# Attention output computed transposed, reciprocals by ln and exp, a modulation spread by matmuls, and a new order: a one-core adaLN block with sliding attention and an MLP

## The chip, the cores and the metric

The kernel runs on one core of a Trainium2 chip. The metric is the device time in microseconds (us) of one execution. TensorE is called PE, VectorE DVE, ScalarE ACT, GpSimd POOL and SyncE SP. SP mostly issues DMAs; ACT issues a few at the start.

## The reference

```python
mod = (_silu(c) @ w_mod).reshape(c.shape[0], 6, 1, -1)
sa, ca, ga, sb, cb, gb = ...
h = _layernorm(x) * (1 + ca) + sa
x = x + ga * _A_ref(h, A_wqkv, A_wo)
h = _layernorm(x) * (1 + cb) + sb
x = x + gb * _B_ref(h, B_w1, B_b1, B_w2, B_b2)

# _A_ref: H = 16 heads of 28; token s looks at the 8 keys s, s-2, ..., s-14
logits = jnp.einsum('bhsd,bhswd->bhsw', q, kg) * scale
attn = _softmax(jnp.where(mask, logits, -1000000000.0))
o = jnp.einsum('bhsw,bhswd->bhsd', attn, vg)        # then o @ wo
# _B_ref: layernorm, gelu(y @ w1 + b1) @ w2 + b2
```

x is 2048 tokens by 448, in bf16; the MLP is 1792 wide. `c` is one row of 448, so the six modulation vectors sa to gb are one row of 448 each.

## The kernel before

**Layout.** Tokens are split by parity, which turns the dilation of 2 into a plain window of 8 within each half of 1024 tokens. They lie in 16 blocks of 128. `hT` (`T.h`) holds the normalized input transposed, with 448 features in four overlapping slices of 128 rows, so that a product over 448 is three full matmuls and one over 64 rows; `pair_mm` (L592 full, L598 half) does two outputs at a time. `qT` and `kT` hold Q and K transposed, each head on a strip of 32 partitions (28 used), four heads m to a slice.

**First norm.** For each pair of blocks: statistics on DVE (L513 to L516), the power -1/2 on POOL (L520), normalization on DVE into `z` (L531). Blocks 0 to 3 are transposed on PE (L547), blocks 4 to 15 by DMA transposes on SP's queue (L539). `modulate` (L564 on ACT, L567 on DVE) then applies 1 + ca and sa.

**Attention.** Q and K come by chunks of 256 or 512 tokens (L592, L598) and are copied out of PSUM by ACT or DVE (L277, L279). Queries go in 36 groups of 57 tokens, four to one of nine rounds called duos. For each duo: 64 logit matmuls (`lt`, L663), four exponentials on ACT (`ex`, L673), two mask multiplies on DVE (`mk`, L680), V for its keys (`v`, L705 and L714) copied on ACT (`ve`, L277), then 64 value matmuls (`pv`, L739) of 29 columns, of which the 29th, a column of ones beside V, gives the sum of the weights. Queries stand on the partitions of that result. DVE takes reciprocals of the sums (`on`, L750) and multiplies (L752); eight transposes on PE (`pt`, L763) and a copy (`ote`, L277 or L279) bring the result back to features by tokens, into `qT`, whose queries are no longer needed. `wo_pair` multiplies two blocks by `wo`, which was scaled by `ga` (L953), and DVE adds x (L796).

**Second half.** Per pair of blocks: statistics and norm, modulation (`g2`, `sb`), statistics and norm again, all on DVE (L814 to L845) with powers on POOL (L822), then a DMA transpose into `hT` (L853). The MLP goes by quarters of 512 tokens: `w1_pairs` (L592, L598 with `w`), gelu on ACT (L880), and `w2_block` (L893, L899). `w2` was scaled by `gb` (L957), and `xp` on POOL (L808) prepares the sum with x. The output is written by DMA (L920).

**The later modulation.** ga, sb, 1 + cb and gb are rows of one PSUM result (`m2`, L932), each repeated on 32 partitions; DVE copies it to `mrow` (L939), and 16 DMAs on SP's queue (L945) spread each row over 128 partitions.

**What sets the order.** Every step is an `Item` with a cost, the engines it may run on, and the buffers it takes from pools (eight PSUM banks `ps`, three exponential buffers `et` and so on). `Plan.schedule` places the items one after another by priorities: a bias and a slope per kind of step, and a table `delta` of single corrections. Each engine then runs its list strictly in that order; waits are by semaphores. Fillers (`fill`, L456) are matmuls on zeros that keep PE busy. A weight load with `lag=3` waits for the load that stands three places ahead of it. Phases are laid out as attention rounds 0 to 6, MLP quarters 0 and 1, rounds 7 and 8, quarters 2 and 3, with ACT's exponentials and gelus kept apart by phase, since they use different tables.

## Time and profile before

| what | value |
|---|---|
| median of 3 runs | 188.39 us (187.07 to 190.14) |
| the profiled execution | 189.24 us, its span 187.5 us |
| mean granted PE clock in it | 0.951 |
| PE busy | 174.8 us, 93% of the span |
| DVE, ACT, POOL busy | 124.2, 92.7, 38.9 us |
| DMA | 16.17 MB moved, 26630 packets |

The profile's busy share of PE counts matmuls at whatever clock was granted, so a slice at half clock looks as full as one at full clock; the row PEclk tells them apart. A mean over the span mixes three stages: the front (to about 18 us), attention (to 87 us, where the first MLP matmul starts) and the rest, in which MLP quarters and the last two attention rounds are woven. The chain of waits names, step by step, what the last instruction waited for; "issue" in it is time that no wait explains, and SPq is SP's sequencer issuing a DMA.

### The profile page before, as it was taken

The numbers are of one execution on the slowest core, as the hardware profiler recorded it, in microseconds if no ns is written. First come the engines' busy times: TensorE is split into PE (matmuls) and PEld (weight loads), VectorE is DVE, ScalarE is ACT, GpSimd is POOL, SyncE is SP. The second block draws the span as 40 slices with busy tenths as digits, with TensorE's granted clock in tenths as the row PEclk, the third lists the DMA queues.
The fourth block names the chain that finished last, engine by engine and source line by source line (L and its number), as shares of the span: only waits on it lengthen the run. The fifth ranks groups of instructions, "written<-read, shape, count | busy, mean of one in ns | idle before, by whom it ended". The sixth has DMA issues, their size and how long they took to land.

```text
span 187.5 us, 5167 instructions
## 1 busy us (share of the span) xinstructions
PE 174.8 (93%) x2151; PEld 85.3 (46%) x2151; DVE 124.2 (66%) x347; ACT 92.7 (49%) x171; POOL 38.9 (21%) x66
## 2 busy tenths in 40 slices
PE   7699998967799999998999999999999999999992
PEld 2445553432224455563344554355554455434562
DVE  4386997676599699999998986006769985200121
ACT  3055927645278876666570405678541720066400
POOL 7211310300061006411311146002203235000000
PEclk9979999995559999999999999999999999999998
DMA  5999999764820200013022120600000042120011
GB/s 176 349 337 329 224 243 164 242 200 100 141 56 3 56 9 0 3 31 31 2 56 56 23 36 7 150 3 0 3 5 0 0 115 77 22 98 0 0 52 49
DMA packets 26630, 16.17 MB, mean 86 GB/s; under 512 B 16045, under 2 KB 26606, under 8 KB 26606
## 3 DMA queue, kind: packets, MB, share of 16 engines
q1 hardware_dynamic: 25918, 14.92, 33.2%
q10 hardware_dynamic: 688, 0.92, 1.5%
q8 instruction: 17, 0.28, 0.6%
q14 instruction: 7, 0.06, 0.1%
HBM read 9.87 MB, written 1.84 MB: 62 GB/s over the span
## 4 chain that ended last, share of the span: by engine, by line
PE 72%; DMA 11%; DVE 6%; SPq 5%; issue 3%; ACT 1%; DVEq 0%
PE ps L592 31%; PE ps L893 21%; PE ps L598 6%; DMA w<-in_B_w_dram 4%; PE ps L705 3%; DMA hm<-in_w_mod_dram 3%; SPq L945 3%; DMA hT<-z 2%; DMA hT<-y 2%; PE ps L739 2%; PE ps L456 2%; DVE st L513 2%; PE ps L663 2%; PE ps L763 2%; PE ps L899 1%
## 5 line engine op out<-in xcount | busy, mean ns | idle before, releaser
L880 ACT ACTIVATE hm<-ps,b1c 128x512 bf16<-128x512 f32 x56 | 34.1, 689 | 45.5 <-PE ps L598 40.6
L893 PE MATMUL ps<-w,hm 128*128 128x448 bf16 x210 | 41.2, 353 | 0.0
L592 PE MATMUL ps<-hT,w 128*128 128x512 bf16 x168 | 38.6, 379 | 0.9 <-DMA hT<-y 0.9
L910 DVE TENSOR_TENSOR x_all<-ps,xp 128x448 bf16<-128x448 f32 (+1 forms) x17 | 9.9, 592 | 36.7 <-PE ps L893 34.7
L808 POOL TENSOR_TENSOR xp<-x_all,gbb 128x448 f32<-128x448 bf16 x16 | 17.2, 1087 | 56.2 <-DVE x_all L796 25.8
L893 PEld LDWEIGHTS <-hm 128*128 128x128 bf16 x210 | 20.1, 98 | 19.1 <-issue 0.8
L592 PE MATMUL ps<-hT,Wqk 128*128 128x512 bf16 (+1 forms) x120 | 25.9, 355 | 2.4 <-DVE hT L567 1.9
L592 PEld LDWEIGHTS <-w 128*128 128x128 bf16 x168 | 15.7, 98 | 21.2 <-issue 3.7
L822 POOL TENSOR_TENSOR rs<-tv,nhalf 128x2 f32<-128x2 f32 x16 | 11.6, 727 | 37.4 <-DVE tv L817 37.1
L673 ACT ACTIVATE et<-ps 128x464 bf16<-128x464 f32 x36 | 17.2, 569 | 3.3 <-PE ps L663 3.2
L592 PEld LDWEIGHTS <-Wqk 128*128 128x128 bf16 x120 | 10.9, 100 | 14.4 <-issue 6.7
L680 DVE TENSOR_TENSOR et<-et,mask 128x928 bf16<-128x928 bf16 x18 | 13.4, 767 | 0.4 <-ACT et L673 0.2
L592 PE MATMUL ps<-wo,qT 128*128 128x448 bf16 x48 | 11.6, 381 | 1.2 <-DVE qT L279 1.2
L705 PE MATMUL ps<-Wv,hT 128*64 128x448 bf16 x108 | 12.5, 374 | 0.0
L277 ACT CAST kT<-ps 128x512 bf16<-128x512 f32 (+1 forms) x18 | 9.3, 522 | 5.7 <-PE ps L598 4.3
L277 ACT CAST vb<-ps 128x448 bf16<-128x448 f32 x18 | 8.8, 536 | 6.2 <-PE ps L714 5.3
L277 ACT CAST qT<-ps 128x512 bf16<-128x512 f32 (+1 forms) x18 | 9.1, 520 | 5.5 <-PE ps L598 4.8
L456 PE MATMUL ps<-zero 128*128 128x512 bf16 x28 | 10.2, 512 | 1.2 <-DVE oz L282 1.2
L520 POOL TENSOR_TENSOR rs<-tv,nhalf 128x2 f32<-128x2 f32 x8 | 5.9, 743 | 25.7 <-DVE tv L516 25.5
L796 DVE TENSOR_TENSOR x_all<-ps,x_all 128x448 bf16<-128x448 f32 x16 | 9.2, 618 | 2.0 <-PE ps L592 2.0
L752 DVE TENSOR_TENSOR on<-ps,rden 128x448 bf16<-128x448 f32 x18 | 10.4, 619 | 0.0
L513 DVE BATCH_NORM_STATS2 st<-x_all 128x6 f32<-128x448 bf16 x16 | 9.2, 615 | 0.8 <-DMA x_all<-in_A_x_dram 0.8
(89 smaller groups left out, 191.7 us busy)
## 6 DMA issues: line engine op xcount, KB each, us to landing
w<-in_B_w_dram SPq DMA_DIRECT2D x6, 448.0 KB, 5.1
hm<-in_w_mod_dram SPq DMA_DIRECT2D x5, 448.0 KB, 4.4
x_all<-in_A_x_dram SPq DMA_DIRECT2D x3, 448.0 KB, 6.5
out_dram<-x_all SPq DMA_DIRECT2D x3, 448.0 KB, 2.8
w<-in_B_w_dram SPq DMA_DIRECT2D x2, 336.0 KB
hm<-in_A_wqkv_dram ACTq DMA_DIRECT2D x1, 448.0 KB
hm<-in_A_wqkv_dram SPq DMA_DIRECT2D x1, 448.0 KB, 6.8
Wv<-in_A_wqkv_dram SPq DMA_DIRECT2D x2, 224.0 KB, 6.7
```

Source lines behind the costliest of these rows:

```text
L277: T.nc.scalar.copy(out=out, in_=in_)
L456: T.nc.tensor.matmul(psf(fvl)[:, 0:512], lhsT=T.zero[:, 0:128], rhs=T.zero[:], start=True, stop=True)
L513: T.nc.vector.bn_stats(out=T.st[:, b, :], in_=T.x[:, b, :])
L592: nc.tensor.matmul(outs[o], lhsT=stat(o, sl, 0, 128), rhs=mov(o, sl, 0, 128), start=(i == 0 and not flip), stop=(i == 2 and flip))
L598: nc.tensor.matmul(outs[o], lhsT=stat(o, sl, lo, lo + 64), rhs=mov(o, sl, lo, lo + 64), start=flip, stop=not flip, tile_position=(lo, 0))
L673: T.nc.scalar.activation(out=T.et[ev.slot][:, r * 464:(r + 1) * 464], in_=psf(lv[r])[:, 0:464], func=ACT.Exp, scale=float(DH) ** -0.5)
L680: T.eng[e].tensor_tensor(out=t, in0=t, in1=T.mask[:], op=ALU.mult)
L705: nc.tensor.matmul(psf(vv[P_])[64 * u:64 * u + 64, 0:D], lhsT=T.h[:, sl, k0:k0 + SK], rhs=T.Wv[:, sl, :], start=(i == 0 and not flip), sto ...
L808: T.eng[e].tensor_tensor(out=T.xp[xpv[b].slot][:], in0=T.x[:, b, :], in1=T.gbb2[:], op=ALU.add)
L822: T.nc.gpsimd.tensor_tensor(out=T.rs2[i][:, bs[0]:bs[0] + 2], in0=T.tv2[i][:, bs[0]:bs[0] + 2], in1=T.nhalf[:, 0:2], op=ALU.pow)
L880: T.nc.scalar.activation(out=T.hm[hmv[q].slot][:, 512 * f:512 * f + 512], in_=psf(v)[:, 0:512], func=ACT.Gelu_apprx_tanh, bias=T.b1c[:, f: ...
L893: T.nc.tensor.matmul(psf(v)[:, 0:D], lhsT=T.hm[hmv[q].slot][:, 512 * f + 128 * (b % 4):512 * f + 128 * (b % 4) + 128], rhs=T.w2[:, f, :], ...
```

## The change

**Output transposed.** Per duo, 16 new matmuls (`dn`) multiply a block of ones, 64 by 32, with the masked exponentials; each gives the sums over the keys for one strip of heads, repeated on 32 partitions, 232 columns wide. The 64 value matmuls now take V (32 columns, of which four are zero) as the stationary operand and the exponentials as the moving one (58 columns), so heads and features stand on partitions and queries along the columns, as the output projection wants them. Two passes on ACT turn the sums into reciprocals, a logarithm from PSUM and an exponential of its negative in place, in fp32; a multiply on DVE writes `qT`. The transposes, the copy behind them and DVE's reciprocals go away. Before a set of exponentials the program loads the table that holds both functions.

```diff
+                        T.nc.tensor.matmul(psf(pd[u])[32 * r:32 * r + 32, P_ * 232:P_ * 232 + 232],
+                                           lhsT=T.one128[64 * u:64 * u + 64, 0:32],
+                                           rhs=T.et[ev.slot][64 * u:64 * u + 64, c0:c0 + 232],
...
+                            T.nc.tensor.matmul(psf(po[u])[32 * r:32 * r + 32, P_ * 232 + m * SC:P_ * 232 + (m + 1) * SC],
+                                               lhsT=T.vb[vbv.slot][64 * u:64 * u + 64, P_, 4 * m + r, :],
+                                               rhs=T.et[ev.slot][64 * u:64 * u + 64, c0:c0 + SC],
...
+                T.nc.scalar.activation(out=T.rec[rv.slot][:], in_=psf(pd[u])[:, 0:464], func=ACT.Ln)
...
+                T.nc.scalar.activation(out=T.rec[rv.slot][:], in_=T.rec[rv.slot][:], func=ACT.Exp, scale=-1.0)
...
+                T.nc.vector.tensor_tensor(out=T.q[:, :, c0:c0 + 2 * SQ].rearrange("p m (a c) -> p m a c", a=2),
+                                          in0=v4(psf(po[u])[:, 0:464]), in1=v4(T.rec[rv.slot][:]), op=ALU.mult)
-                T.nc.vector.reciprocal(out=T.rden[ov[u].slot][:], in_=o3[u][:, :, DH])
-                    T.nc.tensor.transpose(out=t[:, sl, u, :], in_=T.on[ov[u].slot][:, OFF[sl]:OFF[sl] + 128],
```

`wo` is laid out by strips of heads to match (four loads into 28 rows each, after a memset on POOL), and the projection is four full matmuls for each block, block by block:

```diff
+                for m in range(4):
+                    T.nc.tensor.matmul(psf(vs[a])[:, 0:D], lhsT=T.q[:, m, c0:c0 + 128], rhs=T.wo[:, m, :],
-            pair_mm([psf(v)[:, 0:D] for v in vs],
-                    lambda a, sl, lo, hi: T.q[lo:hi, sl, PADL + 128 * bs[a]:PADL + 128 * bs[a] + 128],
-                    lambda a, sl, lo, hi: T.wo[lo:hi, sl, :])
```

**The later modulation.** `mrow` may be copied by ACT; four matmuls of one row each (`bcm`) spread the rows into four PSUM banks, and ACT or DVE copies them out. The 16 DMAs go.

```diff
+            T.nc.tensor.matmul(psf(bvs[j])[:, 0:D], lhsT=T.one128[32 * j:32 * j + 1, :], rhs=T.mrow[32 * j:32 * j + 1, :],
+                               start=True, stop=True, tile_position=(32 * j, 0))
...
+            copy(e, getattr(T, nm)[:], psf(bvs[j])[:, 0:D])
-            for i in range(4):
-                T.nc.sync.dma_start(out=getattr(T, nm)[32 * i:32 * i + 32, :], in_=T.mrow[32 * j:32 * j + 32, :])
```

**V first, and loads.** The first V group is now the front's goal in place of the first Q/K group, whose copies of weights lose that rank. `Wv` is loaded ahead of the Q/K weights and of blocks 2 and 3 of x; both Q/K loads go to SP's queue, and a third part of the first modulation's weights to ACT's. Chunks of 256 tokens put two Q/K results in one PSUM bank, with one copy for both. The mask is spread on POOL alone, and V's padding is set to zero there. The last block is stored in two halves.

**Order.** `delta` is emptied, all biases and slopes are new, `xp` has five buffers instead of six, and the planner gets a penalty per kind for DVE, and a margin by which a more urgent item displaces the next one:

```diff
-CFG["tail"], CFG["slope"], CFG["window"] = 0.0008, 0.0758, 0.03
+CFG["tail"], CFG["slope"], CFG["window"] = 0.0902, 1.0034, 0.03
...
-POOLS = {"ps": 8, "hm": 3, "et": 3, "vb": 3, "on": 4, "z": 6, "y": 4, "z2": 4, "xp": 6}
+POOLS = {"ps": 8, "hm": 3, "et": 3, "vb": 3, "rec": 4, "z": 6, "y": 4, "z2": 4, "xp": 5}
```

What this moves is seen in the engines' lists. SP's queue in the middle of attention, before (`w_76` is w1, `w_77` w2, `z` a normalized block, `b` the second bias):

```order
L539 DMA_TRANSPOSE hT<-z_98 128x4x128
L375 DMA w_76<-in_B_w_dram 128x2x896 x2
L945 DMA ga<-mrow 32x448 x4
L945 DMA sbm<-mrow 32x448 x4
L375 DMA w_76<-in_B_w_dram 128x2x896
L380 DMA w_77<-in_B_w_dram 128x3x448
L945 DMA gb<-mrow 32x448 x4
L945 DMA g_148<-mrow 32x448 x4
L380 DMA w_77<-in_B_w_dram 128x4x448
L539 DMA_TRANSPOSE hT<-z_100 128x4x128
L539 DMA_TRANSPOSE hT<-z_99 128x4x128
```

The same stretch of SP's queue now, from the transpose of block 7 on (`z_92`), with blocks 8 to 11 in `z_93` to `z_96`:

```order
L561 DMA_TRANSPOSE hT<-z_92 128x4x128
L392 DMA b_140<-in_B_b_dram 128x448
L402 DMA w_77<-in_B_w_dram 128x3x448
L397 DMA w_76<-in_B_w_dram 128x2x896
L561 DMA_TRANSPOSE hT<-z_93 128x4x128
L397 DMA w_76<-in_B_w_dram 128x2x896
L561 DMA_TRANSPOSE hT<-z_94 128x4x128
L561 DMA_TRANSPOSE hT<-z_95 128x4x128
L397 DMA w_76<-in_B_w_dram 128x2x896
L561 DMA_TRANSPOSE hT<-z_96 128x4x128
```

The spreading DMAs are gone from between the two halves of the transposes, and the weight loads stand among the transposes. ACT's list in the same stretch, before, from the copies of the Q/K chunk of blocks 4 to 7 to the modulation of later blocks:

```order
L277 CAST kT<-ps_66 128x512
L277 CAST qT<-ps_62 128x512
L277 CAST vb_86<-ps_63 128x16x28
L277 CAST vb_86<-ps_61 128x16x28
L673 ACTIVATE et_83<-ps_64 128x464
L673 ACTIVATE et_83<-ps_65 128x464
L673 ACTIVATE et_83<-ps_66 128x464
L673 ACTIVATE et_83<-ps_68 128x464
L277 CAST vb_84<-ps_62 128x16x28
L277 CAST vb_84<-ps_63 128x16x28
L564 ACTIVATE hT<-hT,mcol 128x512 x2
```

And now (L791 is the logarithm, L796 the exponential of its negative, L587 the modulation of blocks 8 to 11, L294 a copy):

```order
L791 ACTIVATE rec_89<-ps_66 128x464
L796 ACTIVATE rec_89<-rec_89 128x464
L791 ACTIVATE rec_90<-ps_62 128x464
L796 ACTIVATE rec_90<-rec_90 128x464
L294 CAST qT<-ps_61 128x512
L587 ACTIVATE hT<-hT,mcol 128x512
L294 CAST kT<-ps_65 128x512
L294 CAST qT<-ps_67 128x512
L294 CAST ga<-ps_62 128x448
L294 CAST sbm<-ps_68 128x448
L294 CAST g_144<-ps_63 128x448
L294 CAST gb<-ps_61 128x448
```

The modulation now stands ahead of the last copies of the earlier chunk and of the spread vectors. DVE, where the first duo's result is made, before:

```order
L750 RECIPROCAL rden_91<-ps_64 128x16
L750 RECIPROCAL rden_92<-ps_67 128x16
L752 TENSOR_TENSOR on_87<-ps_64,rden_91 128x448
L752 TENSOR_TENSOR on_88<-ps_67,rden_92 128x448
L939 TENSOR_SCALAR mrow<-ps_62,onecol 128x448
L531 TENSOR_SCALAR z_99<-x_all,mv,rs 128x512
L531 TENSOR_SCALAR z_100<-x_all,mv,rs 128x512
L567 TENSOR_SCALAR hT<-hT,mcol 128x512 x3
```

And now:

```order
L805 TENSOR_TENSOR qT<-ps_61,rec_87 128x4x114
L553 TENSOR_SCALAR z_95<-x_all,mv,rs 128x512
L553 TENSOR_SCALAR z_96<-x_all,mv,rs 128x512
L590 TENSOR_SCALAR hT<-hT,mcol 128x512 x3
L805 TENSOR_TENSOR qT<-ps_68,rec_88 128x4x114
```

Each multiply there waits for ACT's `rec`, with the normalizations of blocks 10 and 11 and the modulation behind it.

More of the change, by code (lines that the diff above doesn't have):

```diff
@@ L255 @@
+    "ztp": (-599.25, 0.02),
 }
@@ L263 @@
+CFG['delta'] = {}
+CFG['hold'] = 0.0
+CFG['margin'] = 75.0
+CFG['pen'] = {'bce': 1.44, 'front': 1.16, 'md': -0.48, 'mod2': 0.94, 'qke': -0.14, 've': 0.55, 'wcp': 1.38}
 class Names:
@@ L288, in psb, with fn, load @@
         return T.psb[v.slot]
+    def fn(e):
+        memset(e, T.wo[:], 0.0)
+    add("woz", "cst", {"POOL": 1.0}, fn, wr=[("wo", r) for r in range(4)])
     loads = []
-    def load(name, nbytes, fn, wr, vals=(), n=1, q="SP", lag=0):
+    def load(name, nbytes, fn, wr, vals=(), n=1, q="SP", lag=0, lat=0.9):
         after = [loads[-lag]] if lag else []
@@ L351, in build_plan, with fn @@
         load(f"ldwv{j}", 256 * 896, fn, [("Wv", j)])
+    for j in range(2):
+        def fn(e, j=j):
+            return e.dma_start(**overl(wraw(), T.wqkv, j, 0, 896))
+        load(f"ldwqk{j}", 256 * 896 * 2, fn, [("wraw", j)], vals=[fv])
+    load_x(2, 2)
     load_x(4, 4)
@@ L1076 @@
     with tc.manual_schedule():
+        table = "exp"
         for it in order:
             T.it = it
+            if it.eng == "ACT" and it.kind in TABLE:
+                if TABLE[it.kind] != table and table == "gelu":
+                    nc.scalar.preload_act_table_set(EXP_SET)
+                table = TABLE[it.kind]
             it.fn(it.eng)
```

283 lines of the change are left out of this document (151 added, 132 removed).

## The prediction

> **What bounds the kernel now.** I read the page first: busy shares, then the 40 slices.
>
> ```profile
> PE 174.8 (93%) x2151; PEld 85.3 (46%) x2151; DVE 124.2 (66%) x347; ACT 92.7 (49%) x171; POOL 38.9 (21%) x66
> PE   7699998967799999998999999999999999999992
> ACT  3055927645278876666570405678541720066400
> PEclk9979999995559999999999999999999999999998
> ```
>
> The TensorE (PE) is full from slice 13 on, but slices 7 to 12 hold gaps, and in slices 10 to 12 its granted clock is about half. The windows view sizes this by stage (columns: length, then busy us of PE, PEld, DVE, ACT, POOL, then clock, DMA share, GB/s).
>
> ```profile
> 18.40:87.30 68.90, 62.38 (x1258) 30.43 (x1256) 58.40 (x162) 43.94 (x89) 14.13 (x16) 0.90 0.51 104
> 87.30:184.20 96.90, 96.82 (x774) 46.68 (x774) 54.29 (x141) 41.86 (x68) 18.56 (x21) 1.00 0.15 35
> 57.00:87.30 30.30, 29.40 (x698) 15.56 (x697) 27.95 (x74) 20.93 (x40) 7.22 (x8) 1.00 0.13 21
> 45.00:57.00 12.00, 9.33 (x92) 2.94 (x89) 9.90 (x29) 6.29 (x12) 3.05 (x3) 0.52 0.57 105
> 43.00:44.00 1.00, 1.00 (x10) 0.40 (x6) 0.32 (x1) 0.95 (x3) 0.00 (x0) 0.50 0.14 36
> ```
>
> From 87.3 us, where the first MLP matmul starts, PE runs 96.82 of 96.90 us at full clock: there only less PE work helps. All that can be won otherwise lies in 18.4 to 87.3, the attention stage. PE idles 68.90 - 62.38 = 6.5 us in it; a clock of 0.90 over 68.9 us is some 14 us at half clock, of which 12 - 9.33 = 2.7 us are idle, so (14 - 2.7) / 2 = 5.7 us lost. Why it idles is in the chain of waits (start, length, what), and in the SyncE (SP) queue's own timeline:
>
> ```profile
> 44.66 3.89 DMA hT<-z
> 48.55 1.99 issue
> 51.26 0.81 ACT hT L564
> 52.10 2.29 PE ps L592 x5
> ```
>
> ```profile
> 26.10 1.81 SPq L539 DMA_TRANSPOSE hT<-z  x1
> ...
> 30.96 2.85 SPq L945 DMA_DIRECT2D ga<-mrow  x4
> 33.92 3.87 SPq L945 DMA_DIRECT2D sbm<-mrow  x4
> ...
> 38.98 2.41 SPq L945 DMA_DIRECT2D gb<-mrow  x4
> 41.44 2.49 SPq L945 DMA_DIRECT2D g<-mrow  x4
> 43.98 0.58 SPq L380 DMA_DIRECT2D w<-in_B_w_dram  x1
> 44.66 8.44 SPq L539 DMA_TRANSPOSE hT<-z  x6
> ```
>
> From 30.96 to 44.6 us SP issues 16 small spreading DMAs of the later modulation and three weight loads; the transposes of tokens 1024 to 2047 stand behind them. They are issued from 44.66 us, so the Q/K matmuls of that half start at 51 to 52 us. That block is the present bound of the stage.
>
> **The change, part by part.**
>
> *Spreading by matmuls.* It takes 2.85 + 3.87 + 2.41 + 2.49 = 11.6 us of issue out of SP between two groups of transposes. It adds two more `wo` loads (about 0.5 us each, as the loads above) and one half store at the end. What is late next: the transposes of blocks 8 to 11. The fourth transpose (block 7) ends its issue at 27.9 us now; behind it the new SP order has the bias load, a `w2` load, three `w1` loads, each of which waits for an older load, and those four transposes: 27.9 + 5 x 0.6 + 4 x 1.2 = 35.7 us for the last issue, and a landing near 38.5 (a first one took 3.9 us from issue in the chain above, I take less for the last of four), where now it is 48.55. The loads' waits are the unknown; I take 0, since what they wait for was issued three loads before, and keep the present landing as the other end. The price moves to PE (four matmuls with one row each, bounded by 0.2 us, one 448-column round, and 1.05 us, the 16 matmuls of L932 below; I take 0.3) and to ACT (one `mrow` and four copies).
>
> *Output transposed, ones, ln/exp.* PE rows of one group each:
>
> ```profile
> 63.55 0.55 PE ps L763 x8
> ...
> 72.29 1.26 PE ps L705 x12
> 73.55 0.31 PE ps L714 x4
> 73.86 0.63 PE ps L663 x64
> 74.49 1.24 PE ps L592 x6
> 75.73 0.29 PE ps L598 x2
> 76.03 0.61 PE ps L739 x64
> 22.48 1.05 PE L932 MATMUL ps<-hm,silu_bc 128*32 128x448 bf16 x16
> ```
>
> Removed: nine times 8 transposes, 9 x 0.55 = 5.0 us. The new value product has 64 matmuls of 58 columns like the logits (0.63 us for 64) in place of 64 of 29 columns (0.61): nothing. The 16 matmuls that sum over keys (232 columns) have no row: between 16/64 of 0.63 = 0.16 us and the 1.05 us of L932's 16 matmuls of 448 columns. I take 0.35, nearer to the short ones, since eight fit beside one another as in the logits: 9 x 0.35 = 3.2 us (1.4 to 9.5). The output projection goes from 1.24 + 0.29 = 1.53 us for a pair to eight full matmuls, 8 x 1.24 / 6 = 1.65: +1 us for eight pairs. PE in all: -5.0 + 3.2 + 1.0 + 0.3 = -0.5 us.
> The Trainium skill, "TensorE: Matmul & The Clock Gate", Part 3, gives the span of packed tiles as one matmul's latency and about 4 ns for each further tile; 16 tiles of 232 columns would be an estimate of (398 + 232) / 2.4 + 15 x 4 = 322 ns, and nine groups 2.9 us in place of my 3.2.
>
> VectorE (DVE) and ScalarE (ACT), from the groups (busy us, mean ns) and the ACT timeline:
>
> ```profile
> L750 DVE RECIPROCAL rden<-ps 128x16 f32<-128x16 f32 x18 | 3.3, 223 | 1.4 <-PE ps L739 1.4
> L752 DVE TENSOR_TENSOR on<-ps,rden 128x448 bf16<-128x448 f32 x18 | 10.4, 619 | 0.0
> L279 DVE COPY qT<-ps 128x912 bf16<-128x912 bf16 x6 | 3.8, 637 | 1.3 <-PE ps L763 1.3
> L277 ACT COPY qT<-ps 128x912 bf16<-128x912 bf16 x2 | 1.8, 919 | 1.7 <-PE ps L763 1.7
> 20.42 1.91 ACT L673 ACTIVATE et<-ps 128x464 bf16<-128x464 f32 x4
> 30.24 0.95 ACT L277 CAST vb<-ps 128x448 bf16<-128x448 f32 x2
> 55.94 2.23 ACT L564 ACTIVATE hT<-hT,mcol 128x512 bf16<-128x512 bf16 x3
> ```
>
> DVE loses the reciprocals (3.3) and the copies (3.8); the new multiply has 456 elements from PSUM against 448 and stays at 10.4. ACT gains 36 instructions of 464 elements, priced as the exponentials, 1.91 / 4 = 0.48 us: 17.2 us in all, 28 of them (13.4 us) ahead of the first MLP matmul; also 5 x 0.48 = 2.4 us for spreading. It loses about 3 us of copies and, by the new order, three of six modulations (2.2 us). So in the attention stage ACT goes from 43.9 to about 43.9 + 13.4 + 2.4 - 3 - 2.2 = 54.5 us. That is the dearest part of the change. Added waits: DVE's multiply now waits for PE's sums and then two ACT passes (0.96 us), with later normalizations and three modulations queued behind it; a modulation of blocks 8 to 11 stands on ACT ahead of two copies that the next logits need.
>
> *V first, and the front.* V moves ahead of the first Q/K matmuls while ACT and DVE copy the weights, but with 0.4 us of filler among the first transposes and three fillers behind V. The same V group ran before 18.4 us already, so I take 0 (1 us either way). What holds the front is
>
> ```profile
> 7.77 0.89 PE L489 MATMUL ps<-silu,hm 128*128 128x1 bf16 x30 [1.59 <-DMA hm<-in_w_mod_dram]
> 9.00:10.00 1.00, 1.00 (x9) 0.75 (x8) 0.16 (x1) 0.37 (x1) 0.00 (x0) 0.50 1.09 376
> 41.30 0.67 PE L663 MATMUL ps<-qT,kT 28*64 28x58 bf16 x61 [1.87 <-DVE on L752]
> ```
>
> a load of the first modulation, which moves from SP to ACT's queue; if it lands 1 us earlier, the half clock behind it goes as well, for 2.5 us at most. POOL's longer list of memsets and the mask (some 3 us more) ends before its first results are needed at about 14 us.
>
> *The order.* After the change the attention stage holds about the same PE work: 62.4 busy - 5.7 lost to the clock - 1.8 of filler (0.59 + 1.25, below) = 54.9; six transposes out (-3.3), seven sums in (+2.5), two more output blocks (+1.6), one V group less (-1.26 - 0.31 = -1.6): 54.1 us. DVE has 58.4 - 7 = about 51, ACT 54.5.
>
> ```profile
> 18.40 0.59 PE L456 MATMUL ps<-zero 128*128 128x512 bf16 x2
> ...
> 19.56 1.25 PE L456 MATMUL ps<-zero 128*128 128x512 bf16 x5
> ```
>
> So three engines are all near 54 us, and the stage can't be shorter than that. How much longer? In 57 to 87.3 us, without waits for DMAs, PE was busy 97% with ACT at 69%; here ACT stands at 100% of that floor. From the landing at 38.5 us the new order leaves ACT 37 us of work to the first MLP matmul: 20 exponentials, 20 of ln and exp, 18 Q/K copies, 12 V copies and four spreading copies at 0.48, and two modulations at 2.23 / 3 = 0.74. At 88% busy, midway between 75% and the floor, that takes 42 us: the first MLP matmul at 80.5, against 87.3. The bounds are the floor, 18.4 + 54.5 / 0.97 = 74.6, and the rival on ACT below.
>
> **The sum.** Against the profiled execution: 189.24 us, of which 187.5 are its span; the median of the runs shown is 188.39, 0.85 lower. Front 0; attention stage -6.8; from there PE has 96.9 us less two output blocks (1.6) and three transpose groups (1.65), plus two sums (0.7), one V (1.6): 95.9, -1; I give that 1 us back for DVE, which has the second norms of blocks 4 to 7 to do just as the second quarter's MLP wants them; tail 0. So 189.24 - 6.8 = 182.4 us, and against the median 181.6. I forecast 182.
>
> **Rivals.**
> *ACT takes the bound.* ACT's highest share with no external wait so far is 69% (20.93 of 30.30). If in-order waits between PE, ACT and DVE hold it to 75%, 37 us take 49.3 and the MLP starts at 87.8: 189 us, no change. It decides from about 49 us on. For it speaks the two-pass reciprocal in the middle of DVE's and PE's queues; against it that ACT had nothing more to do in those 30 us.
> *The transposes stay late (slower).* If the weight loads' own waits hold the SP queue without the spreading DMAs, blocks 8 to 11 land at 48.5 as now. Then ACT's 37 us at 88% start there: MLP at 48.5 + 42 = 90.5, 3.2 us later than now, 192.5 us. It decides from a landing at 45.3 on. Against it: only three such loads stand there, and 11.6 us of issue are gone.
> *A new gap with half clock.* The gap of 1.59 us before 7.77 was followed by half clock at 9 us, and that of 1.87 us before 41.30 by half clock from 43 us. If lt (the logits) of the third group waits over 1.6 us for the copies behind ACT's modulation, up to 14 us at half clock return, 5.7 us: 187 us. In "TensorE: Matmul & The Clock Gate", Part 1, the Trainium skill puts the fall to half clock after an idle window of about 3.4 us; by that rule such a gap costs only itself. This trace disagrees, with 1.59 and 1.87 us, so I keep the rival.
> *The front gains too*, 2.5 us and the stage near its floor of 55 us (MLP at 74.6): 189.24 - 12.7 - 2.5 = 174 us.
>
> **Chances.** Forecast case 0.55 (its own range 178 to 186), ACT bound 0.17, late transposes 0.10, new gap 0.10, front and floor 0.08. The range 174 to 190 leaves out the late transposes and the worst of ACT's case. A measurement of this kernel tells about 2% from no change: under 184.6 is faster, over 192.2 slower. Faster: most of the forecast case, the best case and a part of the gap case, 0.66; slower: the late transposes and a little of ACT's, 0.13; the same: 0.21.
>
> **What would show it.** In SP's timeline no L945-like rows and the transposes of blocks 8 to 11 issued by 35 us; no half clock from 42 to 56 us; the first MLP matmul near 80 us and PE full behind it; 72 transposes gone and 144 sum matmuls at about 3 us busy; ACT near 110 us busy, in the stage about 88%, with ln and exp at 0.48 us apart and still four table loads. I am wrong if PE waits for ACT or DVE through 45 to 80 us, if the transposes still land after 45, or if the sums cost near 1 us a group.

## The result, and the profile after

The median of the changed kernel is 187.39 us against 188.56 us of the kernel before, 20 runs each; the ratio is 0.9883 with a 95% interval of 0.9842 to 0.9925. Some executions of either kernel took longer, at a lower clock as a rule, and the ratios leave them out, so they differ from the quotient of the medians, which are over all (0.994 here). A later measurement of the same two gave 0.9964 (0.9916 to 1.0013). So the change gained 1.2% or nothing that can be told from noise; the forecast was 182 us, 3.4% less than before. The profiled execution took 188.89 us, 1.5 us above the median; a second profile of the same kernel, e18 below, is of one that took 186.09 us. I call them the first and the second profile.

The page of the changed kernel first: busy shares, then the slices of PE, ACT and of the granted clock, as shown for the kernel before.

```profile
PE 172.6 (92%) x2227; PEld 84.2 (45%) x2227; DVE 119.4 (64%) x322; ACT 107.8 (58%) x200; POOL 43.3 (23%) x65
...
PE   6799963999699998899999999999999999999992
...
ACT  3086864599769997839385015699835900962000
...
PEclk9999996699879999789999999999999999999999
```

There is no broad hole of half clock in slices 10 to 12 any more; in its place stand three narrower ones, in slices 7 to 8, 11 to 12 and 17 to 18, each behind a dip in PE's row. The PE timeline names them (start, length, what; in brackets the idle time just before and who ended it):

```profile
26.06 0.38 PE L743 MATMUL ps<-Wv,hT 64*64 64x448 bf16 x4
31.06 2.72 PE L615 MATMUL ps<-hT,Wqk 128*128 128x512 bf16 x6 [4.61 <-DVE hT L590]
...
49.48 2.72 PE L821 MATMUL ps<-wo,qT 128*128 128x448 bf16 x8 [1.68 <-ACT kT L294]
...
74.54 0.70 PE L692 MATMUL ps<-qT,kT 28*64 28x58 bf16 x64 [0.68 <-DVE qT L805]
...
75.93 0.74 PE L821 MATMUL ps<-wo,qT 128*128 128x448 bf16 x3 [0.40 <-DVE qT L805]
...
77.39 0.72 PE L781 MATMUL ps<-et,vb 64*32 64x58 bf16 x63 [0.40 <-DVE qT L805]
...
86.38 1.46 PE L615 MATMUL ps<-hT,w 128*128 128x512 bf16 x6
...
89.62 2.75 PE L615 MATMUL ps<-hT,w 128*128 128x512 bf16 x12
```

The dear one is the first. PE is through with the second V group at 26.4 and waits to 31.06 for the modulation of blocks 4 to 7. In the kernel before, the same Q/K chunk started at 29.99 behind 0.86 us:

```profile
29.99 1.62 PE L592 MATMUL ps<-hT,Wqk 128*128 128x512 bf16 x6 [0.86 <-DVE hT L567]
```

In the first profile of the changed kernel PE comes 2.7 us sooner to data that come no sooner, and runs at half clock behind the wait. The same wait took 4.37, 4.81 and 4.77 us in the profiles of e3, e4 and e7 below, which have the same order on SP up to there. In e18 it was short, since the front was later and the data came 2.3 us sooner. There the dear one is the wait of a V group for a k copy on ACT, and the first MLP matmul comes at 83.58:

```profile
28.75 1.56 PE L615 MATMUL ps<-hT,Wqk 128*128 128x512 bf16 x6 [0.63 <-DVE hT L590]
...
40.47 0.76 PE L734 MATMUL ps<-Wv,hT 128*64 128x448 bf16 x6 [2.60 <-ACT kT L294]
...
83.58 1.46 PE L615 MATMUL ps<-hT,w 128*128 128x512 bf16 x6
```

SP's timeline of the first profile shows what stands ahead of the transposes that the first wait is for:

```profile
18.48 0.56 SPq L382 DMA_DIRECT2D wo<-in_A_wo_dram  x1
19.08 2.11 SPq L561 DMA_TRANSPOSE hT<-z  x1
21.24 1.34 SPq L402 DMA_DIRECT2D w<-in_B_w_dram  x1
22.62 0.94 SPq L382 DMA_DIRECT2D wo<-in_A_wo_dram  x2
23.60 0.39 SPq L344 DMA_DIRECT2D x_all<-in_A_x_dram  x1
24.04 3.78 SPq L561 DMA_TRANSPOSE hT<-z  x2
...
35.78 1.20 SPq L561 DMA_TRANSPOSE hT<-z  x1
```

The transposes of blocks 6 and 7 stand behind four loads. The issue of the last of blocks 8 to 11 runs from 35.78 to 36.98, where the forecast had its end at 35.7. ACT comes to their modulation at 40.20 without a wait there. In e18, where that issue ended at 36.16, ACT does wait for them, to 39.13:

```profile
39.13 0.81 ACT L587 ACTIVATE hT<-hT,mcol 128x512 bf16<-128x512 bf16 x1 [2.75 <-DMA hT<-z]
```

From the windows view, the stage (length, busy us of PE, PEld, DVE, ACT, POOL, then clock, DMA share, GB/s), up to the first long run of MLP matmuls:

```profile
17.84:89.62 71.78, 63.88 (x1327) 31.08 (x1327) 58.37 (x151) 54.76 (x108) 14.09 (x15) 0.90 0.48 93
```

I split this stage in the same way for several kernels: idle is its length less PE's busy time, the clock's part is busy time times one less the clock, summed over windows of 1 us, and the rest is PE's work at full clock. The split is good to some 1.5 us: the two kernels with the old order hold the same matmuls but for four small ones, and their work comes out at 56.4 and 57.9.

| kernel | stage, us | idle | lost to the clock | work |
|---|---|---|---|---|
| before (18.93 to 87.31) | 68.4 | 6.5 | 5.5 | 56.4 |
| after (17.84 to 89.62) | 71.8 | 7.9 | 5.9 | 58.0 |
| after, its second profile (e18) | 67.3 | 5.2 | 3.3 | 58.8 |
| spreading alone, old order (e16) | 61.9 | 4.0 | 0 | 57.9 |
| after with SP's old order (e17) | 72.6 | 12.3 | 1.8 | 58.5 |
| after, loads last (e6) | 61.8 | 2.4 | 0 | 59.4 |

Of the two kernels without half clock, the new order (e6) has 1.5 us more of PE's work in this stage than the old (e16): among others 12 output blocks for 8 and eight w1 matmuls, for one V group less; from the end of the stage it takes 2.1 us less (98.1 us for 100.2). What was to go, 12 us of idle time and half clock, is still there, 13.8 us in the first profile and 8.5 in e18.

### The profile page after: what moved, and what is told of

It is laid out like the page before. It is cut to its first block, busy times and chain, and to the rows that moved or that the text cites. A ratio compares the mean times of both kernels' runs of the same rounds, so it can differ in the third digit from the quotient of the medians.

```text
span 187.2 us, 5314 instructions
## 1 busy us (share of the span) xinstructions
PE 172.6 (92%) x2227; PEld 84.2 (45%) x2227; DVE 119.4 (64%) x322; ACT 107.8 (58%) x200; POOL 43.3 (23%) x65
## 4 chain that ended last, share of the span: by engine, by line
PE 74%; DVE 11%; DMA 7%; ACT 5%; issue 1%; POOL 0%; DVEq 0%; ACTq 0%
PE ps L615 28%; PE ps L927 21%; PE ps L821 7%; PE ps L622 6%; DMA hT<-z 5%; PE ps L734 3%; DVE qT L805 2%; PE ps L478 2%; PE ps L781 2%; DVE z L553 1%; PE ps L933 1%; DMA x_all<-in_A_x_dram 1%; PE ps L692 1%; DVE st L848 1%; ACT et L702 1%
## 5 line engine op out<-in xcount | busy, mean ns | idle before, releaser
L914 ACT ACTIVATE hm<-ps,b1c 128x512 bf16<-128x512 f32 x56 | 33.5, 698 | 25.2 <-PE ps L622 25.0
L615 PE MATMUL ps<-hT,w 128*128 128x512 bf16 x168 | 38.5, 379 | 0.0
L856 POOL TENSOR_TENSOR rs<-tv,nhalf 128x2 f32<-128x2 f32 x16 | 13.0, 815 | 52.1 <-DVE tv L851 52.0
L709 DVE TENSOR_TENSOR et<-et,mask 128x928 bf16<-128x928 bf16 x18 | 12.4, 691 | 15.8 <-ACT et L702 15.8
L821 PE MATMUL ps<-wo,qT 128*128 128x448 bf16 x64 | 16.1, 398 | 2.4 <-ACT kT L294 1.7
L805 DVE TENSOR_TENSOR qT<-ps,rec 128x456 bf16<-128x456 f32 x18 | 11.4, 631 | 8.6 <-PE ps L821 3.6
L294 ACT CAST vb<-ps 128x448 bf16<-128x448 f32 x18 | 8.8, 555 | 13.5 <-PE ps L743 13.4
L294 ACT CAST qT<-ps 128x512 bf16<-128x512 f32 x16 | 9.5, 594 | 5.1 <-PE ps L622 3.8
L542 POOL TENSOR_TENSOR rs<-tv,nhalf 128x2 f32<-128x2 f32 x8 | 6.5, 809 | 23.2 <-DVE tv L538 22.1
L796 ACT ACTIVATE rec<-rec 128x464 f32<-128x464 f32 x18 | 10.6, 590 | 0.6
L791 ACT ACTIVATE rec<-ps 128x464 f32<-128x464 f32 x18 | 9.9, 550 | 1.7 <-PE ps L768 1.7
L478 PE MATMUL ps<-zero 128*128 128x512 bf16 x28 | 8.9, 452 | 1.8 <-DVE zero L299 1.8
L821 PEld LDWEIGHTS <-qT 128*128 128x128 bf16 x64 | 6.2, 106 | 9.1 <-issue 3.8
```

The source lines that it names most:

```text
L294: T.nc.scalar.copy(out=out, in_=in_)
L478: T.nc.tensor.matmul(psf(fvl)[:, 0:512], lhsT=T.zero[:, 0:128], rhs=T.zero[:], start=True, stop=True)
L615: nc.tensor.matmul(outs[o], lhsT=stat(o, sl, 0, 128), rhs=mov(o, sl, 0, 128), start=(i == 0 and not flip and o // 2 % nb == 0), stop=(i == ...
L709: T.eng[e].tensor_tensor(out=t, in0=t, in1=T.mask[:], op=ALU.mult)
L805: T.nc.vector.tensor_tensor(out=T.q[:, :, c0:c0 + 2 * SQ].rearrange("p m (a c) -> p m a c", a=2), in0=v4(psf(po[u])[:, 0:464]), in1=v4(T.r ...
L821: T.nc.tensor.matmul(psf(vs[a])[:, 0:D], lhsT=T.q[:, m, c0:c0 + 128], rhs=T.wo[:, m, :], start=(m == 0), stop=(m == 3))
```

## The experiments

Theory L held that loads on SP, ahead of the transposes and on the DMA engines, ate the gain; theory A, that ACT with its ln and exp paces the stage. Names of steps: `zt7` is the transpose of block 7, `ldw1..`, `ldw2.`, `ldwo.` are loads of w1, w2 and wo, `ldx12` the load of blocks 12 to 15 of x, `md12.3` a slice of the modulation of blocks 12 to 15. Most edits move steps in the planned order by the lines that the first diff shows in full.

| run | what | median, us | ratio to before (95%) |
|---|---|---|---|
| e1 | three loads behind block 7 | 191.74 | 1.0158 (1.0083 to 1.0234) |
| e2 | w1, w2 loads last | 183.29 | 0.9713 (0.9640 to 0.9785) |
| e3 | one ACT pass less | 186.92 | 0.9887 (0.9840 to 0.9934) |
| e4 | spreading DMAs back | 195.44 | 1.0366 (1.0305 to 1.0426) |
| e5 | loads don't wait for loads | 185.93 | 0.9940 (0.9875 to 1.0005) |
| e6 | e2, x, wo, bias loads don't wait | 180.78 | 0.9653 (0.9518 to 0.9788) |
| e7 | later modulation of blocks 12 to 15 | 185.08 | 0.9876 (0.9821 to 0.9931) |
| e8 | zeros in the gap | 188.35 | 1.0013 (0.9951 to 1.0075) |
| e9 | before, loads as in e6 | 184.16 | 0.9788 (0.9719 to 0.9856) |
| e10 | e6, one ACT pass less | 179.34 | 0.9567 (0.9541 to 0.9592) |
| e11 | e6, two moves | 182.02 | 0.9711 (0.9687 to 0.9734) |
| e12 | e6, spreading DMAs back | 189.33 | 1.0095 (1.0061 to 1.0128) |
| e13 | before, spreading by matmuls | 182.10 | 0.9678 (0.9603 to 0.9753) |
| e14 | e13, loads as in e6 | 179.73 | 0.9546 (0.9466 to 0.9627) |
| e15 | e6, one of e11's moves | 179.47 | 0.9568 (0.9480 to 0.9657) |
| e16 | e13 again | 181.41 | 0.9655 (0.9590 to 0.9719) |
| e17 | after, SP's old order | 189.88 | 1.0117 (1.0070 to 1.0165) |
| e18 | after again | 188.10 | 0.9964 (0.9916 to 1.0013) |

**e1, three loads behind block 7.**

```diff
     order = P.schedule()
+    for names, ref in (
+            (('ldw20', 'ldwo2', 'ldwo3'), 'zt7'),
+    ):
+        moved = [it for it in order if it.name in names]
+        order = [it for it in order if it.name not in names]
+        i = 1 + [it.name for it in order].index(ref)
+        order[i:i] = moved
```

> Three weight loads (one of w2, two of wo) that stand on SP between the transposes of block 5 and block 6 go behind the transpose of block 7; nothing else moves. Theory L (loads ahead of transposes, on SP and on the DMA engines, ate the gain): the transposes of blocks 6 and 7 are issued 2.3 us earlier, at 21.7 in place of 24.04, and PE's gap of 4.61 us ahead of the Q/K matmuls at 31.06 shrinks to about 2.3; half clock stays, since 1.68 us was enough elsewhere. About 185.2 us against 187.4. Theory A (ACT with its ln and exp paces the stage whatever the loads do): the first MLP matmul stays near 86.4 and the time at 187.4.

Slower by 1.6%, against both. SP's timeline of e1 shows what the loads had hidden:

```profile
19.06 1.35 SPq L561 DMA_TRANSPOSE hT<-z  x1
24.37 0.40 SPq L344 DMA_DIRECT2D x_all<-in_A_x_dram  x1
24.83 3.35 SPq L561 DMA_TRANSPOSE hT<-z  x2
...
28.85 0.93 SPq L382 DMA_DIRECT2D wo<-in_A_wo_dram  x2
33.05 0.36 SPq L392 DMA_DIRECT2D b<-in_B_b_dram  x1
```

SP stood still from 20.4 to 24.4 and from 29.8 to 33.05. The x load waits until the second wo load has landed, the bias load for the fourth: each load waits for the one three before it, and with `wo` split in four that is a much younger one. Moving the work out of the wait left the wait.

**e2, e5, e6: the loads' place and their waits.** e2 puts all w1 and w2 loads behind the last transpose, the last x load behind that of block 5, two wo loads and the bias load behind that of block 7, and DVE's scaling of w2 (`w2s`) later; e5 leaves the order and drops the waits between loads; e6 is e2 without the waits of the other loads. The moves are those of e2 and e6, the other lines those of e6; e5 has an empty list in that place.

```diff
+            (('ldx12',), 'zt5'),
+            (('ldwo2', 'ldwo3', 'ldb2'), 'zt7'),
+            (('ldw101', 'ldw100', 'ldw110', 'ldw111', 'ldw20', 'ldw21', 'ldw22', 'ldw23'), 'zt15'),
+            (tuple(f'w2s{f}' for f in range(14)), 'as5'),
...
-            for a in after:
+            for a in (after if name[:4] in ("ldw1", "ldw2") else ()):
                 T.tc.add_manual_dep(it.ins.ins, a.ins.ins.name, SYNC, reason="one load after another")
```

> All eight loads of w1 and w2 go behind the last transpose of the first modulation (block 15), the last wo loads and the bias behind block 7's, and DVE's scaling of w2 stands later, ahead of the second norm of blocks 4 and 5. Theory L: transposes of blocks 6 to 15 are issued from 21 to 37 us, PE's gap before 31.06 falls to under 2 us and that before 49.48 goes, with it the half clock at 50 to 53; first MLP matmul near 80 (86.4 now), time 181. Theory A: ACT is at 88% from 49.5 on and the first MLP matmul stays within 1.5 us of 86.4: 186 or more. A third way: the MLP then waits for w1 or for the scaled w2, which would show as a gap after 80 us.

> The order of the changed kernel, but no load on SP waits any more for the landing of the load three before it (these waits only pace the loads; the tiles differ). Theory L1 (it is the waits between the loads that hold SP): the transposes of blocks 6 and 7 are issued about 1 us earlier (w2's load took 1.34 us there, others 0.4), those of 8 to 15 up to 3 us earlier, PE's gaps shrink to 3.6 and under 1: 185.5 us against 187.4. Theory L2 (the loads themselves hold SP and the 16 DMA engines, at a share of 1.0 to 1.3 there): the transposes are issued earlier but take as much longer to land, no change, 187.

> The second experiment (all w1 and w2 loads last) without the waits of x, wo and bias loads for older loads: there SP stood from 20.1 to 22.97 ahead of an x load and from 26.97 to 30.25 ahead of the bias load, which each wait for a wo load. Theory L1: block 6's transpose is issued at 20.6 in place of 23.42, PE's gap of 3.33 before 29.78 falls to about 0.5, no half clock from 30 to 34, 180 us against 183.3. L2: the DMA engines have little else there (share 0.4 on average from 20 to 24), so it must agree here. If neither holds and the stage is now limited by PE, DVE and ACT from 46 us on, 182.5.

e2 gave 2.9%, e5 nothing that can be told from the changed kernel, e6 3.5%. Issue of the transposes of blocks 6 and 7 and DVE's modulation of them, in e5:

```profile
21.44 3.91 SPq L561 DMA_TRANSPOSE hT<-z  x2
```

```profile
30.43 1.06 DVE L590 TENSOR_SCALAR hT<-hT,mcol 128x512 bf16<-128x512 bf16 x3 [4.03 <-DMA hT<-z]
```

and in e6:

```profile
20.59 2.67 SPq L561 DMA_TRANSPOSE hT<-z  x2
```

```profile
27.77 1.05 DVE L590 TENSOR_SCALAR hT<-hT,mcol 128x512 bf16<-128x512 bf16 x3
```

In e6 the first MLP matmul starts at 78.02, for 86.38 and 83.58 in the two profiles of the changed kernel:

```profile
78.02 1.46 PE L615 MATMUL ps<-hT,w 128*128 128x512 bf16 x6
```

In e5 they are issued 2.6 us earlier than in the changed kernel's first profile (24.04) and are not modulated earlier (30.59 there; in e18, with an issue at 22.51, at 28.28). In e6, with the weights out of the way, they land in time, and PE's gap is gone; in e10 below, which has the same loads and whose logits start as early as in the changed kernel's first profile, it is 0.23 us. So it is the loads' place that counts, and their waits, by the profiles, once the loads are out of the way: e2 still has a gap of 3.33 us there. How the loads make the transposes land late is not shown. The DMA engines' share from 20 to 31 us does not tell e5 from e6 (1.18 and 1.21); the bytes moved do (223 and 144 GB/s).

**e3, e10: one ACT pass less.**

```diff
-                T.nc.scalar.activation(out=T.rec[rv.slot][:], in_=psf(pd[u])[:, 0:464], func=ACT.Ln)
+                T.nc.scalar.activation(out=T.rec[rv.slot][:], in_=psf(pd[u])[:, 0:464], func=ACT.Exp, scale=-1.0)
...
-                T.nc.scalar.activation(out=T.rec[rv.slot][:], in_=T.rec[rv.slot][:], func=ACT.Exp, scale=-1.0)
+                pass
```

> Leaves out one of the two ACT passes of the reciprocal (the result is exp of minus the sum, not one over it): ACT loses 18 instructions of 0.55 to 0.59 us, 14 of them (8 us) ahead of the first MLP matmul. Theory A: the first MLP matmul comes 5 us or more earlier, and the time is 182 or less. Theory L: the gaps of 4.61 and 1.68 us before 31.06 and 49.48 wait for transposes and stay; only part of the 1.5 us of gaps at 74 to 77 goes, 186 us.

> The sixth experiment (180.8 us) without one of the two ACT passes of the reciprocal (the result is exp of minus the sum). ACT loses 18 instructions of 0.55 us. With the transposes early, ACT was 89% busy from 30 to 80 us there. If ACT is what limits the stage now: 4 us or more less, 176.5. If PE is (97% busy from 30 to 80): at most the gaps of 0.74 + 1.2 us go, 179.5 to 181.

e3 took 8 us off ACT ahead of the MLP (46.7 us busy in the stage for 54.8) and left the ratio at 0.9887 (0.9883 and 0.9964 for the changed kernel). On top of e6, e10's stage took 61.6 us for 61.8. Its median is 1.4 us lower, and that lies ahead of the stage: the profiled e6 started it at 19.51, e10 at 17.86 (the last section tells why). Theory A falls in both places: 18 passes of 0.55 to 0.59 us less on ACT do not change the length of the stage beyond the spread of two profiles of one kernel (69.7 us in e3, for 71.8 and 67.3).

**e4, e12: the spreading DMAs back in the new order.**

```diff
+            (('bcga', 'bcsb', 'bcg2', 'bcgb'), 'ldw23'),
...
+    order = [it for it in order if it.name != "bcm"]
...
+            def fn(e, j=("ga", "sb", "g2", "gb").index(it.name[2:]), nm=it.name[2:]):
+                for i in range(4):
+                    T.nc.sync.dma_start(out=getattr(T, nm)[32 * i:32 * i + 32, :], in_=T.mrow[32 * j:32 * j + 32, :])
+            it.fn, it.eng = fn, "SP"
```

> Undoes one part of the change alone: the four matmuls and four copies that spread the later modulation are left out, and the 16 spreading DMAs stand on SP again, ahead of the transposes of blocks 8 to 15. Theory L: SP issues those transposes 10 us later, near 42, they land near 48, the Q/K matmuls of that half start at 51 in place of 43.8, and the time is 194 us. The rival that this part gave nothing (the DMA engines at a share of 1.0 to 1.3 to 45 us would land them late anyway): within 1 us of 187.4.

> The sixth experiment with the 16 spreading DMAs back on SP ahead of the transposes of blocks 8 to 15, in place of the four matmuls and four copies. Theory: their issue (10 us) is what the spreading by matmuls took off the path; the transposes of blocks 8 to 15 are issued from 36 in place of 25.8, the modulation of blocks 8 to 11 comes at 46 in place of 36, and the time is 8 to 10 us more, 189 to 191. Rival: with the loads gone SP has time to spare, 183 or less.

8 us more in e4 (6.6 were expected), 8.5 us in e12, as expected. In both, PE's longest wait is that of a V group for a k copy on ACT, 10.06 and 8.74 us. In the new order the spreading by matmuls is worth about 8 us, so either the old order paid less for the DMAs, or something else in the change gives 7 us back.

**e7, e8: the second gap, and the clock.**

```diff
+            (('md12.0', 'md12.1', 'md12.2'), 'w2s8'),
+            (('md12.3',), 'ke3.1'),
```

```diff
+                for i in range(20 if (t0, ms[0]) == (512, 0) else 0):
+                    T.nc.tensor.matmul(psf(vs[0])[:, 0:512], lhsT=T.zero[:, 0:128], rhs=T.zero[:], start=True, stop=True)
```

> The changed kernel, but the modulation of blocks 12 to 15 stands two copies later on ACT (behind the k copy that frees a PSUM bank) and behind five scalings of w2 on DVE. Loads as in the changed kernel. If in-order ACT made the gap of 1.68 us at 49.48 and the half clock behind it, both go: 1.7 + 1.3 us, 184.5 against 187.4. If what PE gains there it loses later (ACT or DVE full up to 87), the gap goes and the time stays: 187.

> The changed kernel with 20 matmuls of zeros (0.22 us each) ahead of the Q/K matmuls at 31.06, in a bank that is free, so that PE isn't idle while it waits for the transposes. Theory C (the half clock from 31 to 37 is on the path, some 3 us of it): 184.5 us; the transposes are as late as before. Rival: PE then only waits sooner for the transposes of blocks 8 to 11 (modulated at 40.2) or of 12 to 15 (48.2), the Q/K matmuls at 43.77 and 51.99 don't move by more than 1 us, and the time is 187.

e7's gap at 49 us is gone. Its ratio is 0.9876, for 0.9883 and 0.9964 of the changed kernel, so whether that gained anything stays open. e8 kept the clock full from 30 to 40 us and was no faster: PE waited behind the modulation of the next blocks instead, 1.03 us ahead of 41.89 and 1.04 us ahead of 48.98, and the Q/K matmuls that had started at 43.77 started at 43.92. (Its zeros ran to 32.4, 1.4 us past the start of the modulation that the chunk waits for, so they cost some of what they won.) Here half clock behind a wait for data was no cost of its own, since the next data were late too.

**e9: the loads in the old kernel.** The load lines of e6 in the kernel before (`zt14` is its last transpose).

> The kernel before with its loads as in the sixth experiment: all w1 and w2 loads behind the last transpose of the first modulation, the x, wo and bias loads without their waits, DVE's scaling of w2 later. The 16 spreading DMAs stay ahead of the transposes of blocks 10 to 15. If the loads only became the limit when the spreading DMAs were gone (theory L): those DMAs still hold SP some 10 us, the transposes behind them are issued at 38 in place of 44.66 at best and the ACT and DVE instructions that wait for them still hold PE; 185 to 188 us against 188.4. If the loads' place is worth as much without the change (rival: the gain is the loads', the change gives nothing): 182 or less.

Between the two: 2.1% faster. The change with these loads (e6) is 1.4% under it, and with the old loads 1.2% under the kernel before. So the loads' place is worth about as much without the change, and theory L alone does not explain why the change gave little. This left the question of e4: what gives 7 us back?

**e13, e14, e16: the spreading alone, in the old order.** One matmul and one ACT copy for each row, behind the copy `ke2.0`, in four PSUM banks (PE waits 1.05 us, ahead of 36.54 in e16, for one of these copies to free its bank):

```diff
+            (('bcga', 'bcsb', 'bcgb', 'bcg2'), 'ke2.0'),
...
+                p = T.ps[banks[nm]][:, 0:D]
+                nc.tensor.matmul(p, lhsT=T.one128[32 * j:32 * j + 1, :], rhs=T.mrow[32 * j:32 * j + 1, :],
+                                 start=True, stop=True, tile_position=(32 * j, 0))
+                nc.scalar.copy(out=getattr(T, nm)[:], in_=p)
```

> The kernel before with one part of the change alone: the later modulation is spread by four matmuls and four ACT copies in place of the 16 DMAs, everything else in its old order. Theory S (the spreading is the whole gain, the other parts only move work): about the changed kernel's ratio, 0.985 to 0.99 of before, 186 us. Rival O (in the old order the late transposes were mostly covered by other PE work, so that the spreading gives nothing there, and the new order is needed): 188 or more. Rival G (the other parts give back what the spreading wins): clearly under the changed kernel, 183 or less.

> The same with all w1 and w2 loads behind the last transpose and without the waits of the x, wo and bias loads. Theory S: as the sixth experiment, 0.965 of before, 181. Rival O: as the ninth experiment, 0.979, 184. Rival G: 178 or less.

> The thirteenth experiment again (the kernel before with the spreading by matmuls alone), for its profile, on the same chip as the next two. Rival G holds if it stays at 0.965 to 0.975 of before, with the transposes of blocks 8 to 15 done on SP by about 40 us and no half clock after 40; at 0.985 or more the thirteenth run was a lucky one and Theory S holds.

0.9678 and again 0.9655: the spreading alone gives 3.4%, and the rest of the change gives two thirds of it back, or more: 187.95 us became 181.41 in e16, and the changed kernel took 188.10 beside it (e18). (The profiled execution of e13 took 921 us and shows nothing of the kernel; e16's is used.) With the loads last, e14 reaches 0.9546, 1.1% under e6, which is within their intervals. So it seems that most of what the rest of the change gives back is paid where loads stand among the transposes.

**e17, e18: SP's old order in the changed kernel.**

```diff
+            (('ldwo0',), 'zt4'),
+            (('ldx12',), 'zt6'),
+            (('ldwo2', 'ldwo3'), 'zt7'),
+            (('ldb2',), 'ldwo3'),
+            (('ldw23',), 'zt8'),
+            (('ldw100', 'ldw110', 'ldw111', 'ldw21', 'ldw22'), 'zt9'),
```

The x, wo and bias loads go without their waits, as in e6.

> The changed kernel with its SP queue in the order of the kernel before (a wo load behind block 4's transpose, x between those of blocks 6 and 7, two wo loads behind block 7's, w1 and w2 loads between those of blocks 9 and 10), x, wo and bias loads without waits; engines as in the changed kernel. If the new order of the SP queue gave back what the spreading won: 0.968 to 0.975, some 183 us, and PE's gap before 31.06 under 2 us. If the order of the work on PE, ACT and DVE did: as the changed kernel, 187, and the gap ahead of the Q/K matmuls of blocks 4 to 7 stays.

> The changed kernel as it is, beside the two above on the same chip: 0.984 to 0.993 of before, as measured at first.

e17 is slower still (1.0117 for 0.9964 beside it): the order on SP is not what gave the gain back. e16 and e17 have nearly the same queue on SP, and ACT modulates blocks 8 to 11 at the same time in both. ACT in e16, where two V copies run up to it:

```profile
41.25 1.93 ACT L674 ACTIVATE et<-ps 128x464 bf16<-128x464 f32 x4
43.20 0.97 ACT L277 CAST vb<-ps 128x448 bf16<-128x448 f32 x2
44.05 1.53 ACT L565 ACTIVATE hT<-hT,mcol 128x512 bf16<-128x512 bf16 x2
```

and in e17, where ACT stands ahead of it, with a k copy behind:

```profile
37.43 0.59 ACT L294 CAST qT<-ps 128x512 bf16<-128x512 f32 x1 [0.63 <-DVE qT L805]
44.16 0.81 ACT L587 ACTIVATE hT<-hT,mcol 128x512 bf16<-128x512 bf16 x1 [6.14 <-DMA hT<-z]
44.88 0.56 ACT L294 CAST kT<-ps 128x512 bf16<-128x512 f32 x1
```

What PE does in these microseconds, e16:

```profile
40.25 0.70 PE L664 MATMUL ps<-qT,kT 28*64 28x58 bf16 x64
40.89 0.62 PE L764 MATMUL ps<-ident,on 128*128 128x128 bf16 x8
41.44 1.33 PE L706 MATMUL ps<-Wv,hT 128*64 128x448 bf16 x12
42.69 0.38 PE L715 MATMUL ps<-Wv,hT 64*64 64x448 bf16 x4
43.01 1.31 PE L593 MATMUL ps<-wo,qT 128*128 128x448 bf16 x6
...
45.23 1.64 PE L593 MATMUL ps<-hT,Wqk 128*128 128x512 bf16 x6
...
78.99 2.75 PE L593 MATMUL ps<-hT,w 128*128 128x512 bf16 x12 [1.12 <-ACT vb L277]
```

and e17:

```profile
38.73 0.76 PE L734 MATMUL ps<-Wv,hT 128*64 128x448 bf16 x6
45.49 1.33 PE L734 MATMUL ps<-Wv,hT 128*64 128x448 bf16 x6 [6.00 <-ACT kT L294]
...
47.99 2.00 PE L615 MATMUL ps<-hT,Wqk 128*128 128x512 bf16 x6
...
90.46 2.75 PE L615 MATMUL ps<-hT,w 128*128 128x512 bf16 x12
```

The old order has logits, a V group and a pair of output blocks ready for PE while the transposes of blocks 8 to 11 are under way, and ACT's modulation stands behind the copies that these need. The new order has the modulation in front of the k copy that frees a PSUM bank, so V, and all of PE behind it, waits for a DMA. It suits transposes that land early; with loads between them they don't.

**e11, e15: towards a faster kernel.**

```diff
+            (('md12.3',), 'ke3.1'),
+            (('on3.0', 'on3.1'), 'bs1'),
```

> The sixth experiment, with ACT's modulation of blocks 12 to 15 two copies later and DVE's two products of the fourth group ahead of a mask. PE's gap of 0.74 us at 44.23 goes and of the 1.2 us at 67 to 70 about a half: 179.6 us against 180.8, if PE carries the stage; no change if ACT or DVE do.

> The sixth experiment with the modulation of blocks 12 to 15 two copies later on ACT, and nothing else. PE's gap of 0.74 us at 44.23 goes; if the loss of the eleventh experiment came from the moved DVE products alone, 180 us or a little less; if it came from this move, 182.

e11, with both moves, is clearly behind e15, with the first alone (0.9711 and 0.9568); from e6 neither can be told by the intervals. The loss came from the second move: PE then waited 1.89 us for these products ahead of 63.66, where e6 waited 0.37 us, later on. The two fastest kernels that compute the whole reference are e15, the change with late loads, and e14, the old order with spreading by matmuls and late loads: 179.5 and 179.7 us, which can't be told apart.

## Why the prediction was wrong

- **What bounds the kernel: right.** The block of spreading DMAs was the bound of the stage. Taken away alone it gives 6.5 us (187.95 to 181.41, e16). That this is near the -6.8 us forecast for the stage is luck: those were worked out from ACT's pace in the whole change. (Behind that block stood blocks 10 to 15; 8 and 9 were ahead of it.)
- **Spreading by matmuls: right.** The issue of the last transpose of blocks 8 to 11 ended at 36.98, in e18 at 36.16 (forecast 35.7), in e18 they landed at 39.1 (38.5), and the four matmuls took 0.37 us (0.3). The loads' waits, taken as 0, were there: 4 us and 3.3 us long in e1, which moved three loads out of them; in the changed kernel other loads fill most of that time. What the step did not look at is the pair before: blocks 6 and 7, behind four loads, made the first gap, 4.61 us (0.63 in e18).
- **Output transposed: its prices were right.** 16 sums took 0.32 us in the rows of the chain (forecast 0.35), a pair of output blocks 1.62 (1.65), ACT rose by 15.1 us. e3 shows that one of the two ACT passes is not on the path; what the new form as a whole gains or costs was not measured.
- **V first, and the front: 0 can't be told from what came.** The logits started 1.1 us earlier in the first profile (17.84 for 18.93), and PE reached the chunk of blocks 4 to 7 2.7 us earlier, to wait for it; in e18 they started 0.6 us later (19.52), behind half clock in the front.
- **The order: the step that failed.** It put the first MLP matmul at the landing, 38.5, plus 37 us of ACT's work at 88%, which is 42 us: 80.5. It came at 86.38, and at 83.58 in e18. The work was sized right: ACT was busy 37.27 us from the landing at 39.13 to there in e18. But that took 44.45 us, and in the first profile there are 47.9 us from 38.5 on. ACT does not set the pace, for with one pass less on it the stage is as long (e3, e10). PE does, and it stands still in its order: in the first profile 4.61 us for the modulation of blocks 4 to 7, 1.68 us behind ACT's modulation of blocks 12 to 15, and 1.5 us for DVE's multiplies, with 5.9 us lost to the clock; in e18 2.60 us behind ACT's modulation of blocks 8 to 11, with 3.3 us lost. For these waits the sum had no term beside ACT's 88%. With the loads behind the transposes and the x, wo and bias loads without their waits (e6), PE idles 2.4 us in all, the first MLP matmul comes at 78.02, earlier than forecast, and the ratio is the forecast one, 0.9653 (182 is 0.966 of 188.39).
- **What of it the prediction knew.** It named one such wait ("a modulation of blocks 8 to 11 stands on ACT ahead of two copies that the next logits need") and had the outcome as its rival "a new gap with half clock", 187 us, at 0.10. In the sum it took the new order to bear late transposes as the old one does: the old order bears a modulation of these blocks at 44 us (e16), the new one lost 6.00 us by it (e17). That the other parts together give back 2% or more while the loads stand among the transposes is shown (e16 against the changed kernel); that the engines' order is all of it is not: the new order with the old form of the output was not tried.

## What to carry to other kernels

When a transfer is late, look at what the bound engine has in its queue while it waits: an order with independent work ahead of the wait bears a lateness that the "better" order turns into idle time. Change one part alone before judging a change of several: here one part was worth 3.4% and the rest cost 2 to 3%. Weights that are needed 40 us later belong behind the transfers that are needed now; a wait that paces loads should be looked up again whenever loads are split or moved.

## What the runs showed of the hardware

The clock can fall behind two short gaps. Two profiles of the same changed kernel differ in the front; the first, and then the second (e18):

```profile
7.35 0.89 PE L511 MATMUL ps<-silu,hm 128*128 128x1 bf16 x30 [0.76 <-DMA hm<-in_w_mod_dram]
8.45 0.40 PE L569 MATMUL ps<-ident,z 128*128 128x128 bf16 x4 [0.21 <-DVE z L553]
...
17.84 0.70 PE L692 MATMUL ps<-qT,kT 28*64 28x58 bf16 x64
```

```profile
6.89 0.89 PE L511 MATMUL ps<-silu,hm 128*128 128x1 bf16 x30 [0.49 <-DMA hm<-in_w_mod_dram]
8.44 0.50 PE L569 MATMUL ps<-ident,z 128*128 128x128 bf16 x4 [0.66 <-DVE z L553]
...
19.52 0.70 PE L692 MATMUL ps<-qT,kT 28*64 28x58 bf16 x64
```

In the second the weights of the first modulation land 0.46 us earlier, PE then idles longer ahead of the transposes (1.16 us in all from 6 to 9 us, for 0.97), the clock is at half from 9 to 12 us, and the logits start 1.7 us later. Idle time alone does not decide it: in e6 and e8, with 1.24 and 1.29 us idle from 6 to 9 us, the clock is at half from 9 to 11 us, and in e17, with 1.29 us, it is full. Nor does one gap's length: that of 1.53 us ahead of 48.37 in e5 had no half clock behind it, that of 1.68 us ahead of 49.48 in the changed kernel had. By the granted clock in windows of 1 us, the stretches at half clock last 3.4 us (8.6 to 12.0 and 42.7 to 46.1 in e18, 49.9 to 53.4 in the first profile) or a multiple of it: 6.8 us (29.5 to 36.3), and 13.7 us in the kernel before (42.9 to 56.5).

The Trainium skill, "TensorE: Matmul & The Clock Gate", Part 1, has an idle window of about 3.4 us ahead of the fall to half clock, and has it run free of the program. That the same code falls or not from run to run agrees, and so do the lengths of the stretches. That a whole idle window is needed for the fall does not agree: 1.16 us of idle time was enough in e18.
